# Split products for heads 4 to 11, SP's loads in program order, weights requested six chunks ahead, two weight splits per slot

## Chip, core and metric

The kernel runs on one core of a Trainium2 chip. The metric is the device time of one execution in microseconds (us). TensorE is called PE here, its weight loads PEld, VectorE DVE, ScalarE ACT, GpSimd POOL and SyncE SP.

## What is computed

Windowed attention with global tokens, followed by a two-layer MLP, all in float32. Eight batches, eight heads of 64; 512 local and 32 global tokens. A local token sees the local tokens within 32 places and all global ones; a global token sees everything.

```python
s_g = scale * q_g @ k_all^T;  out_g = softmax(s_g) @ v_all        # k_all, v_all: global and local
s_l = concat(scale * q_l @ k_g^T, where(|i - j| <= 32, scale * q_l @ k_l^T, -1e9))
out_l = softmax(s_l) @ concat(v_g, v_l)
x = concat(out_g, out_l)                  # 8 * 544 tokens, 512 wide
h = maximum(x @ w_in, 0)                  # w_in 512 x 2048
out = (h * h) @ w_out                     # w_out 2048 x 512
```

## The kernel before

**Slots.** The attention is cut into 128 "heads": one head of one batch over one half (256) of its local queries. The loop over t (line 587) handles one head per slot: scores, softmax, transposes of the probabilities, the product with V, and the copy into x. Sixteen heads (two halves of eight) belong to one batch. The MLP follows LAG = 9 slots behind: slot t does step m = t - 9, an eighth of DFF (256 columns) for a block of 256 tokens: gemm1 into h, relu and square, gemm2 into o. Block 0's GEMM reads xg, block 1's x_h and x_l, and so on. In this order block 0 is the group of the first eight heads of batch 0; its eight steps stand in slots 9 to 16. A step of block 0 needs heads 0 to 7 in xg and four chunks of weights.

**Plain and split products.** A float32 product is either plain (operands in float32) or split: an operand is written as hi (rounded to float32r) plus lo (the rest), and the products hi*hi, lo*hi, hi*lo are summed. Heads 0 to 15 (`NPLAIN = 16`, `plain(t)`) and block 0's GEMMs are plain in before, everything later is split. For a split head, `split_head` makes hi with a cast on ACT and the rest with subtractions on DVE. In the buffers of the scores the 64 channels of Q and K stand twice, one copy in each half of the 128 partitions; a plain product therefore gives twice the score and is scaled by 0.0625 instead of 0.125, and a split one keeps hi in the lower and lo in the upper copy of K.

**Global queries.** Every four heads `g_load` loads global queries (qr) and spreads them into a tile of zeros: on POOL into qz for plain heads, with a cast on ACT and a subtraction on DVE into qgz for split ones. `g_scores` multiplies it with K into gs, `g_evac` copies gs into sg. Softmax, transposes and product of the global rows follow as jobs in later slots.

**Weights.** w_in and w_out come as 32 chunks wr of 512 KB in which each float32 number is stored in the two halves of an int64. A chunk is put together by an absolute-value pass on ACT (`w_abs`, ACTIVATE wf<-wr) and two bit passes on DVE (`w_bits`, TENSOR_SCALAR and SCALAR_TENSOR_TENSOR wf); each letter b in `PLAN` is one of a chunk's two bit passes. It is then split into whi and wlo (tile ws, one cast on ACT and one subtraction on DVE) for the blocks after the first: each letter s is one. `PLAN[t]` has four places in slot t. `w_start` asks for chunks up to `LOOK` ahead of the one that is being put together. Weights and plain heads share one pool of 32 buffers of 4 KB per partition.

**Sizes of loads.** A head (raw) is 432 KB, of head 0 first 304 and then 128; half of the masks (con) is 224 KB, the identity 64, the global queries qr 64, a chunk 512.

**What sets the order.** `InOrder` wraps an engine's calls and asks the scheduler to keep them in program order where its flag is on. PE, DVE and ACT get that flag from slot 17 (`FREE`). Before that, and for SP throughout in before, the scheduler chooses an order by its own estimate of times when the kernel is built. On the chip each engine then runs its instructions in the order that was chosen, and waits at an instruction whose operands aren't there.

Of the kernel before, what the change touches and what calls it, by code (L numbers as in the profile page):

```python
# [16 lines left out]
P = 128  # L17
# [10 lines left out]
NPLAIN = 16  # L28

PLAN = [",,,b", "b,,,b", "b,,,b", "b,,b,", "b,,b,", "b,,b,", "b,,b,", "b,b,,b", "b,b,,b", "bb,bb,bb,bb", "bb,bb,bb,bb", "bbs,bb,bbs,bbs", "bbs,bbs,bbs,bbs", "bbs,bbs,bbs,bbs", "bbs,bbs,bs,s", "ss,s,s,s", "ss,s,s,s", "s,,s,", "s,,s,", "s,,s,", "s,,s,", "s,,s,", "s,,s,"]  # L30
FREE = (17, 17, 17)
LOOK = 2
# [26 lines left out]
def attention_moe(  # L59
# [10 lines left out]
    pe, ve, ac = InOrder(tc, nc.tensor), InOrder(tc, nc.vector), InOrder(tc, nc.scalar)  # L70
    PSUM = bass.MemoryType.PSUM
# [12 lines left out]

    w_bufs = {"free": WCH}
# [4 lines left out]
    def load_head(t):  # L90
        if plain(t):
            w_take(1)
            raw = wp.tile([P, 1024], F32, tag="w", name=f"raw{t}")[:, :PK]
        else:
            raw = p2.tile([P, PK], F32, tag="raw", name=f"raw{t}")
        if t == 0:
            nc.sync.dma_start(raw[:, : QC + KC], pk[t, :, : QC + KC])
        else:
            nc.sync.dma_start(raw, pk[t])
        heads[t] = dict(raw=raw)  # L100
# [162 lines left out]
    def g_load(t):  # L263

        b, grp = t // 16, (t // 4) % 2

        def cols(z, j):
            return bass.AP(z.tensor, z.offset + 64 * j, [list(z.ap[0]), [256, 2], [160, 2], [1, 32]])

        src = qg[b, grp].rearrange("p (a b) n -> p a b n", a=2)  # L270
        if plain(t):
            qz = p1.tile([P, 512], F32, tag=("ph", "gvl", "gvh", "ph")[t // 4], name=f"qz{t}")
            nc.gpsimd.memset(qz, 0.0)
            qr = p1.tile([P, 2, 2, 32], F32, tag="qr", name=f"qr{t}")
            (nc.sync if t else nc.scalar).dma_start(qr, src)
            nc.gpsimd.tensor_copy(cols(qz, 0), qr)
        else:
            qz = qgz
            qr = p1.tile([P, 2, 2, 32], F32, tag="qr", name=f"qr{t}")
            nc.sync.dma_start(qr, src)  # L280
            ac.copy(cols(qgz, 0), qr)
            ve.tensor_sub(cols(qgz, 1), qr, f(cols(qgz, 0)))
        state["qz"] = qz

    def g_scores(t):
# [4 lines left out]
        kk = hd["raw" if plain(t) else "hi"]  # L290
# [8 lines left out]
    def g_evac(t):  # L299
        grp, pair = (t // 4) % 2, (t % 4) // 2  # L300
        gs = state["gs"]
        early = plain(t)
# [7 lines left out]
    def g_load_v(t, pair):  # L310
        gv = p1.tile([P, 640], F32, tag="gv", name=f"gv{t}_{pair}").rearrange("p (c n) -> p c n", c=5)
        src = vg[t // 16, 2 * ((t // 4) % 2) + pair]
        nc.sync.dma_start(gv, src.rearrange("(c p) n -> p c n", p=P))
        state["gv"] = gv
# [11 lines left out]
    def g_soft(t):  # L326
# [174 lines left out]
    def evac(blk, tiles=(0, 1)):  # L501
        for i in tiles:
# [76 lines left out]
    for t in range(4, 8):  # L579
# [3 lines left out]
        if t == 6:  # L583
            nc.sync.dma_start(con[:, half:], consts[:, half:])
    scores(0)
    jobs = {}
    for t in range(NSTEP + LAG + 1):
# [40 lines left out]
        if early and t + 1 < NPLAIN:  # L628
            scores(t + 1)
# [11 lines left out]
        if t + 1 < NT:  # L641
# [126 lines left out]
```

## Time and profile before

| | before |
|---|---|
| median of 3 runs (us) | 1073.42 (1073.36 to 1074.84) |
| the profiled execution (us) | 1073.67 |
| its span, first to last instruction (us) | 1071.9 |
| PE, PEld busy (us) | 1055.3, 939.3 |
| DVE, ACT busy (us) | 856.9, 752.2 |
| granted PE clock | 1.0 throughout |

Busy times are sums over instructions of one engine. A matmul's end is modelled in them, and PE works on several at once, so a busy PE may still have room: what PE really takes for a piece is the distance to the next start, as the chain of waits gives it. In a timeline row stand the start, the length, the engine, the line, the operation with its output and inputs, and how many instructions were merged; a plain float32 matmul is two rows. Line 52 is the wrapper of `InOrder`, so operations are told apart by their tiles: s and gs scores, pt transposes, xa and gxo attention products, h and o the two GEMMs.

### The profile page before, as it was taken

Reading aid. Unit: us, or ns where it says so; the run is one execution under the profiler, and the core shown is the slowest. Engines: PE = TensorE matmul, PEld = TensorE weight load, DVE = VectorE, ACT = ScalarE, POOL = GpSimd, SP = SyncE. Lnnn points to the kernel's source line nnn. Section 1 sums busy time; section 2 is a strip of 40 time slices with the busy share of each in tenths; the row PEclk is TensorE's granted clock in tenths of the full one; section 3 lists DMA queues with packets and bytes.
Section 4 is the critical chain, followed back from the end, with each engine's and each line's share of the span. In section 5 each row is a group of like instructions: output and inputs, shape, how many; then the busy total and the mean of one; then the engine's idle time right before and its main releaser. Section 6 shows DMA issues by size and latency. Waiting matters only on the chain.

```text
span 1071.9 us, 21142 instructions
## 1 busy us (share of the span) xinstructions
PE 1055.3 (98%) x7568; PEld 939.3 (88%) x7568; DVE 856.9 (80%) x2687; ACT 752.2 (70%) x1901; POOL 3.9 (0%) x14
## 2 busy tenths in 40 slices
PE   7999999999999999999999999999999999999998
PEld 5676789998999899999998989998999999999896
DVE  4689889888888888888888889888888888884321
ACT  5789776778767776777777776777777787774322
POOL 1000000000000000000000000000000000000000
PEclk9999999999999999999999999999999999999999
DMA  9662222232322222223222222222322322201000
GB/s 372 265 256 92 83 82 82 75 91 76 93 70 82 85 82 66 89 66 102 75 90 65 84 84 82 76 79 83 94 74 69 87 93 65 88 29 34 13 20 20
DMA packets 54312, 96.78 MB, mean 90 GB/s; under 512 B 4288, under 2 KB 29376, under 8 KB 54208
## 3 DMA queue, kind: packets, MB, share of 16 engines
q1 hardware_dynamic: 53632, 94.95, 27.1%
q8 instruction: 60, 0.98, 0.4%
q10 hardware_dynamic: 576, 0.49, 0.2%
q14 instruction: 44, 0.36, 0.1%
HBM read 86.51 MB, written 8.91 MB: 89 GB/s over the span
## 4 chain that ended last, share of the span: by engine, by line
PE 88%; ACT 5%; DVE 3%; DMA 3%; issue 1%; SPq 0%
PE o L52 34%; PE h L52 33%; PE xa L52 7%; PE s L52 5%; PE pt L52 5%; PE gxo L52 2%; PE gs L52 2%; DMA wr<-in_w_dram 1%; DVE prob L52 1%; ACT r L52 1%; ACT ph L52 1%; DMA raw<-in_pk_dram 1%; ACT prob L52 1%; PE gt L52 1%; ACT hi L52 1%
## 5 line engine op out<-in xcount | busy, mean ns | idle before, releaser
L52 PE MATMUL h<-x_h,ws 128*128 128x256 f32 x2048 | 388.8, 283 | 0.0
L52 PEld LDWEIGHTS h<-x_h,ws 128*128 128x128 f32 x2048 | 327.0, 191 | 0.5
L52 PE MATMUL o<-ws,gh 128*128 128x512 f32 x1024 | 321.3, 395 | 0.0
L52 PE MATMUL h<-x_l,ws 128*128 128x256 f32 x1024 | 289.1, 282 | 0.1
L52 PEld LDWEIGHTS o<-ws,gh 128*128 128x128 f32 x1024 | 185.5, 188 | 34.6
L52 PE MATMUL o<-ws,gl 128*128 128x512 f32 x512 | 202.6, 396 | 0.0
L52 PEld LDWEIGHTS h<-x_l,ws 128*128 128x128 f32 x1024 | 195.8, 191 | 0.9 <-DVE x_l L52 0.4
L52 ACT CAST ph<-pt 128x256 fp32r<-128x256 f32 x448 | 141.1, 341 | 68.1 <-PE pt L52 61.2
L52 ACT ACTIVATE prob<-prob,st 128x224 f32<-128x224 f32 x270 | 127.7, 476 | 62.1 <-DVE st L52 60.1
L52 ACT ACTIVATE r<-h 128x512 f32<-128x512 f32 x136 | 81.4, 599 | 112.4 <-PE h L52 112.3
L52 PEld LDWEIGHTS o<-ws,gl 128*128 128x128 f32 x512 | 96.2, 188 | 22.7
L52 DVE CUSTOM_DVE_ANT_0 prob<-s,con 128x224 f32<-128x224 f32 x256 | 89.8, 386 | 25.6 <-PE s L52 19.5
L52 DVE TENSOR_TENSOR gl<-r,gh 128x512 fp32r<-128x512 f32 x128 | 87.9, 686 | 22.3 <-ACT gh L52 20.5
L52 ACT CAST hi<-raw 128x864 fp32r<-128x864 f32 x112 | 102.5, 915 | 1.3
L52 DVE TENSOR_TENSOR r<-h,r 128x512 f32<-128x512 f32 x82 | 56.7, 692 | 52.3 <-ACT r L52 51.0
L52 PE MATMUL xa<-ph,hi 128*64 128x128 f32 x448 | 87.3, 238 | 1.6 <-DVE ph L52 1.2
L52 DVE TENSOR_TENSOR hi<-raw,hi 64x352 fp32r<-64x352 f32 x224 | 82.5, 368 | 6.5
L52 ACT CAST gh<-r 128x512 fp32r<-128x512 f32 x128 | 79.1, 618 | 8.9 <-DVE r L52 8.6
L52 DVE TENSOR_TENSOR ph<-pt,ph 64x128 fp32r<-64x128 f32 x224 | 79.6, 356 | 7.0
L52 DVE TENSOR_TENSOR lo<-raw,hi 128x448 fp32r<-128x448 f32 x112 | 69.7, 622 | 15.2 <-ACT hi L52 12.5
L52 PE MATMUL pt<-con,prob 128*128 128x128 f32 (+1 forms) x512 | 77.9, 274 | 0.1
L52 DVE TENSOR_SCALAR prob<-prob,st 128x224 f32<-128x224 f32 x242 | 70.5, 334 | 4.2
(80 smaller groups left out, 1570.4 us busy)
## 6 DMA issues: line engine op xcount, KB each, us to landing
raw<-in_pk_dram SPq DMA_DIRECT2D x127, 432.0 KB, 3.3
wr<-in_w_dram SPq DMA_DIRECT2D x32, 512.0 KB, 7.4
gv<-in_vg_dram SPq DMA_DIRECT2D x32, 320.0 KB, 3.2
out_dram<-ot SPq DMA_DIRECT2D x32, 256.0 KB, 2.2
qr<-in_qg_dram SPq DMA_DIRECT2D x31, 64.0 KB, 2.7
out_dram<-ot SPq DMA_DIRECT2D x8, 64.0 KB, 1.7
raw<-in_pk_dram SPq DMA_DIRECT2D x1, 304.0 KB, 4.1
con<-in_consts_dram ACTq DMA_DIRECT2D x1, 224.0 KB, 3.9
```

The lines of the kernel that those rows point to most:

```text
L52: r = method(*args, **kwargs)
```

## The change

Heads 4 to 11 (`SCORES`) make their scores and group scores from split operands; their values and the product with V stay plain (`whole(t)` is plain without these heads). Their `split_head` works on 608 columns instead of 864 and is called one slot ahead of the head, right before the scores. Their group queries are qgz on ACT and DVE instead of qz on POOL, and `g_evac` adds two halves on DVE for them; for whole heads it multiplies by 0.5, so that all rows of sg have the same scale. SP's calls go through `InOrder` with its flag always on. `LOOK` is 6 instead of 2. `PLAN` gives two letters s per slot in slots 11 to 14, where 3, 4, 4 and 4 stood, and goes on with two per slot through slot 23 instead of 22.

```diff
+SCORES = range(4, 12)
-PLAN = [..., "bbs,bb,bbs,bbs", "bbs,bbs,bbs,bbs", "bbs,bbs,bbs,bbs", "bbs,bbs,bs,s", "ss,s,s,s", "ss,s,s,s", "s,,s,", ...]
+PLAN = [..., "bbs,bb,bbs,bb", "bbs,bb,bbs,bb", "bbs,bb,bbs,bb", "bbs,bb,b,s", "ss,s,s,s", "ss,s,s,s", "s,,s,", ...]
-LOOK = 2
+LOOK = 6
...
+    sp = InOrder(tc, nc.sync)
...
+    def whole(t):
+        return plain(t) and t not in SCORES
...
-            nc.sync.dma_start(raw, pk[t])
+            sp.dma_start(raw, pk[t])
...
-        if plain(t):
+        if whole(t):
             return
         hi = p2.tile([P, PK], F32R, tag="hi", name=f"hi{t}")
         lo = p2.tile([P, QC + 192], F32R, tag="lo", name=f"lo{t}")
-        ac.copy(hi, raw)
-        ve.tensor_sub(lo, raw[:, KC : KC + QC + 192], f(hi[:, KC : KC + QC + 192]))
+        e = KC + QC if plain(t) else PK
+        n = min(e - KC, QC + 192)
+        ac.copy(hi[:, :e], raw[:, :e])
+        ve.tensor_sub(lo[:, :n], raw[:, KC : KC + n], f(hi[:, KC : KC + n]))
         ve.tensor_sub(hi[64:, :KC], raw[64:, :KC], f(hi[64:, :KC]))
-        ve.tensor_sub(hi[32:64, PK - 64 :], raw[32:64, PK - 64 :], f(hi[32:64, PK - 64 :]))
+        if not plain(t):
+            ve.tensor_sub(hi[32:64, PK - 64 :], raw[32:64, PK - 64 :], f(hi[32:64, PK - 64 :]))
...
-            if plain(t):
+            if whole(t):
                 pe.matmul(s[:, u, :], hd["raw"][:, qs], hd["raw"][:, ks], start=True, stop=True)
...
-        return 0.0625 if plain(t) else 0.125
+        return 0.0625 if whole(t) else 0.125
...
-        if plain(t):
+        if whole(t):
             qz = p1.tile([P, 512], F32, tag=("ph", "gvl", "gvh", "ph")[t // 4], name=f"qz{t}")
...
-        kk = hd["raw" if plain(t) else "hi"]
+        kk = hd["raw" if whole(t) else "hi"]
...
-            ac.copy(dst, gs[:64, cols] if early else gs[64:, cols])
+            if early:
+                ac.activation(out=dst, in_=gs[:64, cols], func=AF.Copy, scale=0.5)
+            else:
+                ac.copy(dst, gs[64:, cols])
...
         if early and t + 1 < NPLAIN:
+            split_head(t + 1)
             scores(t + 1)
...
-        if t + 1 < NT:
+        if NPLAIN <= t + 1 < NT:
             split_head(t + 1)
```

What the scheduler makes of it stands in the built programs. In their rows the number right behind a tile's name is the head, the chunk or, for gs, the first head of a pair; the number behind the underscore only tells buffers apart.

SP's loads behind head 3, before:

```order
L99 DMA raw4_104<-in_pk_dram 128x864
L404 DMA wr0_106<-in_w_dram 128x1024
L404 DMA wr1_108<-in_w_dram 128x1024
L584 DMA con_78<-in_consts_dram 128x448
L99 DMA raw5_112<-in_pk_dram 128x864
L99 DMA raw6_114<-in_pk_dram 128x864
L99 DMA raw7_117<-in_pk_dram 128x864
L99 DMA raw8_122<-in_pk_dram 128x864
```

and now:

```order
L53 DMA raw4_104<-in_pk_dram 128x864
L53 DMA wr0_106<-in_w_dram 128x1024
L53 DMA wr1_108<-in_w_dram 128x1024
L53 DMA wr2_110<-in_w_dram 128x1024
L53 DMA wr3_112<-in_w_dram 128x1024
L53 DMA wr4_114<-in_w_dram 128x1024
L53 DMA wr5_116<-in_w_dram 128x1024
L53 DMA raw5_120<-in_pk_dram 128x864
L53 DMA raw6_122<-in_pk_dram 128x864
L53 DMA con_78<-in_consts_dram 128x448
L53 DMA raw7_125<-in_pk_dram 128x864
L53 DMA raw8_130<-in_pk_dram 128x864
```

Four more chunks stand ahead of heads 5 to 8, and con behind head 6.

PE behind the transposes of head 3 (pt<-prob1), before:

```order
L52 MATMUL s6_302<-raw6_114 128x224 x2
L52 MATMUL s7_337<-raw7_117 128x224
L52 MATMUL xa3_266<-pts3_251,raw3_86 64x256
L52 MATMUL xa3_266<-pts3_251,raw3_86 64x128 x2
L52 MATMUL pt_95<-con_78,prob0_93 128x128 x2
L52 MATMUL pt_95<-con_78,prob0_93 96x128 x2
L52 MATMUL s7_337<-raw7_117 128x224
L52 MATMUL h0_425<-xg_90,wf0_110 128x256
```

and now, from the attention product of head 5 on:

```order
L53 MATMUL xa5_362<-pts5_347,raw5_120 64x256
L53 MATMUL xa5_362<-pts5_347,raw5_120 64x128 x2
L53 MATMUL gs4_278<-hi4_238,qgz_92 128x288
L53 MATMUL gs4_278<-hi5_284,qgz_92 128x288
L53 MATMUL s6_328<-hi6_323 128x224
L53 MATMUL s6_328<-hi6_323,lo6_324 128x224
L53 MATMUL s6_328<-hi6_323 128x224
L53 MATMUL s6_328<-hi6_323,lo6_324 128x224
L53 MATMUL gs6_360<-hi6_323,qgz_92 128x288
L53 MATMUL s7_371<-hi7_366 128x224
```

The scores of heads 6 and 7, ahead of the attention product of head 3 before, stand behind that of head 5 now, and behind the group scores of heads 4 and 5, which read qgz.

DVE behind the probabilities of head 5 (TENSOR_SCALAR prob1), before:

```order
L52 TENSOR_SCALAR prob1_94<-prob1_94,st5_287 128x224 x2
L52 ISA prob0_93,st6_320<-s6_302,con_78 128x224
L52 ISA st6_320 128x1
L52 ISA prob0_93,st6_320<-s6_302,con_78 128x224
L52 ISA st6_320 128x1
L52 TENSOR_SCALAR st6_320<-st6_320 128x2
```

and now:

```order
L53 TENSOR_SCALAR prob1_94<-prob1_94,st5_308 128x224 x2
L53 TENSOR_SCALAR wf2_198<-wf2_198 128x512
L53 SCALAR_TENSOR_TENSOR wf2_198<-wr2_110,wf2_198 128x512
L53 TENSOR_SCALAR wf2_198<-wf2_198 128x512
L53 SCALAR_TENSOR_TENSOR wf2_198<-wr3_112,wf2_198 128x512
L53 TENSOR_SCALAR wf4_276<-wf4_276 128x512
L53 TENSOR_TENSOR qgz_92<-qr4_254,qgz_92 128x2x2x32
L53 SCALAR_TENSOR_TENSOR wf4_276<-wr4_114,wf4_276 128x512
L53 TENSOR_SCALAR wf4_276<-wf4_276 128x512
L53 SCALAR_TENSOR_TENSOR wf4_276<-wr5_116,wf4_276 128x512
L53 TENSOR_TENSOR lo6_324<-raw6_122,hi6_323 128x256
L53 TENSOR_TENSOR hi6_323<-raw6_122,hi6_323 64x352
```

The bits of chunks 2 to 5, qgz and the split of head 6 now stand between head 5's probabilities and the scan (ISA) of head 6's scores.

More of the change, by code (lines that the diff above doesn't have):

```diff
@@ L28 @@
 NPLAIN = 16
-PLAN = [",,,b", "b,,,b", "b,,,b", "b,,b,", "b,,b,", "b,,b,", "b,,b,", "b,b,,b", "b,b,,b", "bb,bb,bb,bb", "bb,bb,bb,bb", "bbs,bb,bbs,bbs", "bbs,bbs,bbs,bbs", "bbs,bbs,bbs,bbs", "bbs,bbs,bs,s", "ss,s,s,s", "ss,s,s,s", "s,,s,", "s,,s,", "s,,s,", "s,,s,", "s,,s,", "s,,s,"]
+SCORES = range(4, 12)
+PLAN = [",,,b", "b,,,b", "b,,,b", "b,,b,", "b,,b,", "b,,b,", "b,,b,", "b,b,,b", "b,b,,b", "bb,bb,bb,bb", "bb,bb,bb,bb", "bbs,bb,bbs,bb", "bbs,bb,bbs,bb", "bbs,bb,bbs,bb", "bbs,bb,b,s", "ss,s,s,s", "ss,s,s,s", "s,,s,", "s,,s,", "s,,s,", "s,,s,", "s,,s,", "s,,s,", "s,,s,"]
 FREE = (17, 17, 17)
-LOOK = 2
+LOOK = 6
 SQ = (2, 3, 4, 5, 14, 15)
@@ L96, in load_head @@
         if t == 0:
-            nc.sync.dma_start(raw[:, : QC + KC], pk[t, :, : QC + KC])
+            sp.dma_start(raw[:, : QC + KC], pk[t, :, : QC + KC])
         else:
-            nc.sync.dma_start(raw, pk[t])
+            sp.dma_start(raw, pk[t])
         heads[t] = dict(raw=raw)
@@ L274, in g_load @@
             qr = p1.tile([P, 2, 2, 32], F32, tag="qr", name=f"qr{t}")
-            (nc.sync if t else nc.scalar).dma_start(qr, src)
+            (sp if t else nc.scalar).dma_start(qr, src)
             nc.gpsimd.tensor_copy(cols(qz, 0), qr)
@@ L279, in g_load @@
             qr = p1.tile([P, 2, 2, 32], F32, tag="qr", name=f"qr{t}")
-            nc.sync.dma_start(qr, src)
+            sp.dma_start(qr, src)
             ac.copy(cols(qgz, 0), qr)
@@ L301, in g_evac @@
         gs = state["gs"]
-        early = plain(t)
+        early = whole(t)
         parts = ((0, 0, 288),) if (t // 8) % 2 == 0 else ((288, 0, 160), (448, 192, 96))
@@ L312, in g_load_v @@
         src = vg[t // 16, 2 * ((t // 4) % 2) + pair]
-        nc.sync.dma_start(gv, src.rearrange("(c p) n -> p c n", p=P))
+        sp.dma_start(gv, src.rearrange("(c p) n -> p c n", p=P))
         state["gv"] = gv
@@ L329, in g_soft @@
         ve.tensor_reduce(out=st[:, 0:1], in_=s[:, :544], op=ALU.max, axis=AX.X)
-        ve.tensor_scalar(out=st[:, 1:2], in0=st[:, 0:1], scalar1=-scale(t), scalar2=None, op0=ALU.mult)
+        ve.tensor_scalar(out=st[:, 1:2], in0=st[:, 0:1], scalar1=-0.125, scalar2=None, op0=ALU.mult)
         state["gst", t] = st
@@ L334, in g_exp @@
         s, st = sg[:, (t // 4) % 2, :544], state["gst", t]
-        ac.activation(out=s, in_=s, func=AF.Exp, scale=scale(t), bias=st[:, 1:2], accum_out=st[:, 2:3])
+        ac.activation(out=s, in_=s, func=AF.Exp, scale=0.125, bias=st[:, 1:2], accum_out=st[:, 2:3])
     def g_norm(t):
@@ L403, in w_load @@
         r = wp.tile([P, 1024], F32, tag="w", name=f"wr{i}")
-        nc.sync.dma_start(r.bitcast(I32), w[i].bitcast(I32))
+        sp.dma_start(r.bitcast(I32), w[i].bitcast(I32))
         wraw[i] = r.rearrange("p (n w) -> p n w", w=2)
@@ L508, in evac @@
                 r0 = b * 544 + 32 + hf * 256 + i * P
-                nc.sync.dma_start(out[r0 : r0 + P, :], ot)
+                sp.dma_start(out[r0 : r0 + P, :], ot)
             else:
@@ L512, in evac @@
                     r0 = (4 * i + bb) * 544
-                    nc.sync.dma_start(out[r0 : r0 + 32, :], ot[32 * bb : 32 * bb + 32, :])
+                    sp.dma_start(out[r0 : r0 + 32, :], ot[32 * bb : 32 * bb + 32, :])
     w_next = {"load": 0, "bits": 0, "split": 0}
@@ L583, in attention_moe @@
         if t == 6:
-            nc.sync.dma_start(con[:, half:], consts[:, half:])
+            sp.dma_start(con[:, half:], consts[:, half:])
     scores(0)
```

## The prediction

> **What bounds the kernel now.** I read the page's engine shares first, then the busy time in stretches of the start, then PE's waits there, then the chain of work in one slot.
>
> ```profile
> span 1071.9 us, 21142 instructions
> core 0: us, PE busy (x) PEld busy (x) DVE busy (x) ACT busy (x) POOL busy (x), PEclk, DMA share, GB/s
> 20.00:30.00 10.00, 9.65 (x56) 7.18 (x56) 6.65 (x35) 7.39 (x23) 0.29 (x1) 1.00 1.03 411
> 30.00:40.00 10.00, 9.60 (x50) 6.74 (x49) 7.74 (x34) 8.54 (x25) 0.59 (x2) 1.00 1.04 406
> ...
> PE s L52 <- DMA raw<-in_pk_dram: 4.9, 1, 4.9
> ...
> PE xa L52 <- DVE ph L52: 1.1, 7, 0.2
> PE s L52 <- ACT sg L52: 0.9, 6, 0.2
> ...
> 59.99 3.43 PE o L52 x8
> 63.42 0.44 PE pt L52 x4
> 63.86 1.73 PE h L52 x8
> 65.58 0.49 PE gs L52 x2
> 66.07 1.73 PE h L52 x8
> 67.80 1.01 PE xa L52 x6
> 68.81 0.95 PE s L52 x4
> ```
>
> The first row of waits is PE's only one for a load in the first 50 us, at the very start; the next two are all its waits behind 190 us, 2.0 us together. The last seven rows are the chain through slot 11. They add up to 9.78 us with no gap: from the first GEMM slots onwards PE sets the pace, and whatever lets the first GEMM begin later moves all that follows by as much. Before that, heads 0 to 7 must go through softmax into xg. In that stretch no engine is full (DVE 6.65 and 7.74 of 10, ACT 7.39 and 8.54) while the DMA engines are (share 1.03, 411 GB/s). So the start is made of waits in a chain, not of work on PE, and the order of the built program decides it.
>
> **Products of heads 4 to 11.** A plain score pair or group score costs what the slot above shows (s 0.95, gs 0.49 us); a split one costs what later slots show:
>
> ```profile
> 103.66 0.44 PE s L52 x4
> 125.41 0.13 PE gs L52
> ```
>
> That saves about 0.5 + 0.36 us of PE a head. Only what stands behind the first output product (o) counts in full, since PE is the bound from there. That is the group score of head 11, 0.36 us. (The group scores of whole heads leave ACT with a factor now instead of none, which is the same pass: nothing, or the width of a reading either way.) The rest lies in the stretch that the next part walks through. Where PE is the bound from about 31 us, as in the second rival, the three scores and eight group scores behind that point give 3 x 0.5 + 8 x 0.36 = 4.4 us.
>
> **The order in the start: the term that decides.** The rows that price the steps are the groups of the first 190 us, with their mean ns behind the comma:
>
> ```profile
> L52 DVE SCALAR_TENSOR_TENSOR wf<-wr,wf 128x512 int32<-128x512 int32 x32 | 22.0, 688 | 0.5
> L52 DVE TENSOR_SCALAR wf<-wf 128x512 int32<-128x512 int32 x32 | 13.8, 431 | 9.5 <-ACT wf L52 9.2
> L52 DVE TENSOR_TENSOR hi<-raw,hi 64x352 fp32r<-64x352 f32 x11 | 5.7, 522 | 0.3
> L52 DVE TENSOR_TENSOR pl<-pt,ph 128x256 fp32r<-128x256 f32 x10 | 4.2, 421 | 0.1
> L52 DVE CUSTOM_DVE_ANT_0 prob<-s,con 128x224 f32<-128x224 f32 x54 | 19.4, 386 | 15.8 <-PE s L52 10.3 <-PE pt L52 5.3
> L52 DVE TENSOR_SCALAR prob<-prob,st 128x224 f32<-128x224 f32 x40 | 11.6, 334 | 0.6
> ...
> L52 ACT ACTIVATE prob<-prob,st 128x224 f32<-128x224 f32 x68 | 31.8, 477 | 19.1 <-DVE st L52 18.8
> L52 ACT ACTIVATE wf<-wr 128x512 f32<-128x512 f32 x32 | 21.4, 669 | 1.2 <-DMA wr<-in_w_dram 1.2
> L52 ACT CAST ws<-wf 128x512 fp32r<-128x512 f32 x32 | 18.6, 615 | 0.0
> L52 ACT COPY pts<-pt 128x512 f32<-128x512 f32 x16 | 9.3, 580 | 2.9 <-PE pt L52 2.8
> L52 ACT CAST gvh<-gv 128x640 fp32r<-128x640 f32 x4 | 2.9, 723 | 0.0
> ```
>
> Neighbours on DVE and ACT overlap by some 0.08 us (below, 0.42 us from 31.73 and the next from 32.07), so I count a chunk's bits on DVE as 1.05, its absolute value on ACT as 0.6, and the split of a head as 0.65 on ACT (608 columns, between the ws and gvh rows) and 0.9 on DVE (the 128x256 and 64x352 rows). A step to another engine counts 0.1.
>
> ```profile
> 31.73 0.42 DVE L52 TENSOR_SCALAR wf<-wf 128x512 int32<-128x512 int32 x1
> 32.07 0.38 DVE L52 CUSTOM_DVE_ANT_0 prob<-s,con 128x224 f32<-128x224 f32 x1
> ...
> 23.09 1.30 PE L52 MATMUL s<-raw 128*128 128x224 f32 x6
> ...
> 25.34 0.66 PE L52 MATMUL pt<-con,prob 128*128 128x128 f32 x4
> ...
> 30.69 0.79 PE L52 MATMUL pt<-con,prob 128*128 128x128 f32 x4
> ...
> 37.78 0.43 PE L52 MATMUL xa<-pts,raw 128*64 128x128 f32 x2
> ...
> 50.05 3.60 PE L52 MATMUL o<-wf,r 128*128 128x512 f32 x8
> ```
>
> These are the marks of before: scores of head 6 from 23.09 (a product in plain float32 is two rows), transposes of head 4 at 25.34, of head 6 at 30.69, the last attention product of head 7 ending at 38.2, the first output product at 50.05. Now the same marks in the changed order:
>
> - Up to head 4's transposes the rows are nearly the same, and its split fits into gaps of ACT and DVE: 25.1.
> - Head 5's scores now stand behind head 4's attention product. Copy of the transposes, cast, two subtractions: 28.0. Softmax, with 2 x 0.386 on DVE, 2 exponentials on ACT, 2 x 0.334 on DVE and the small steps between, takes 3.7: transposes at 31.7.
> - Head 6's scores stand on PE behind the group scores of heads 4 and 5, which now wait for DVE's half of qgz. On DVE both qgz and head 6's split stand behind the bits of chunks 2 to 5. ACT delivers the first of these at 33.55 (pts and two absolute values); DVE then needs 4 x 1.05 + 0.25 for qgz + 0.9 for head 6: 38.95, and the scores run at 39.05. Before, they ran at 23.09, ahead of all this. (qgz is 128 columns, so under the 0.33 us that 224 columns take in the prob row.)
> - Until head 6's probabilities are ready DVE runs through a group sum 0.4 (288 columns, near the 0.42 of the 256 above), head 7's split 0.9, head 6's scan 0.75 and its factor 0.15, head 8's split 0.9, half of chunk 6's bits 0.43, head 7's scan 0.75, three small steps 0.3, the other half 0.6, the product 0.58: 5.76 us, so 44.7. Before: 30.69 for the transposes.
> - Another 3.3 us of DVE of the same kinds to head 7's probabilities, 48.05; ACT has chunks 8 and 9, half of head 8's exponentials, xg and the second qgz ahead of the copy; head 7's attention product ends at 51.1, against 38.2.
> - Until the first o PE has 8.6 us of work (4.3 of h0 and h1 and the rest in scores, transposes and products of heads 8 to 11), with ACT's order (three absolute values, a cast, pts, exponentials, r and its square, x_h, the multiplication on ACT) holding it up in two places by some 3.2 us: 62.85, against 50.05.
>
> The term is **+12.8 us**. Bounds: with another 8% of overlap on the 26 us that DVE and ACT carry in it, and no time for steps between engines, 9; with 0.2 instead of 0.1 for each of about 20 steps, 15. Behind PE's waiting group score stand all scores from head 6 on; DVE's scans wait for those, and h0 for head 7.
>
> **Loads.** SP issues six chunks before heads 5 to 8, instead of two.
>
> Four chunks of 512 KB at 411 GB/s are 5.1 us. From the first landing at 4.9 us, the 5,500 KB up to and with head 5 are here by 18.6, and heads 6 to 9, with half of con and 1,950 KB in all, by 23.5. The walk needs head 5 at 26 and the others later, so this costs nothing in it; it would cost up to 5.1 if that slack were gone. The Trainium skill's page "Perfetto Trace Analysis", section Roofline, says that a lone core is bounded by its 16 DMA engines at about 435 GB/s; the trace's 411 and 406 GB/s at a share of 1.03 and 1.04 agree with the ceiling. By that rule alone the start would be loading-bound and would pay the 5.1 us; the first rival below takes this up.
>
> **Splits later.** Slots 11 to 14 lose seven splits. They are bound by PE (9.78 above), so nothing is won. Slots 21 to 23 get two each that were done by slot 20 before; one more in slot 17 finds room.
>
> ```profile
> 136.79:146.57 9.78, 1.38 (x2) 1.00 0.33 100
> ...
> 128.17:136.79 8.62, 7.96 (x59) 7.14 (x58) 8.12 (x26) 7.81 (x20) 0.00 (x0) 1.00 0.18 53
> 136.79:146.57 9.78, 9.08 (x70) 7.66 (x69) 8.73 (x26) 7.72 (x19) 0.00 (x0) 1.00 0.33 100
> 146.57:154.10 7.53, 7.53 (x59) 6.87 (x58) 6.22 (x22) 5.88 (x15) 0.00 (x0) 1.00 0.31 102
> 154.10:161.46 7.36, 7.36 (x57) 6.73 (x56) 6.62 (x22) 5.34 (x13) 0.00 (x0) 1.00 0.18 61
> 161.46:169.50 8.04, 8.04 (x69) 7.45 (x68) 7.64 (x23) 5.24 (x14) 0.00 (x0) 1.00 0.33 98
> ```
>
> The first row is DVE's part of ws alone in slot 20: two splits are 1.38 us. The others are slots 19 to 23. Added to DVE's 6.22, 6.62 and 7.64 they make 7.60, 8.00 and 9.02 in slots of 7.53, 7.36 and 8.04: over by 0.07, 0.64 and 0.98, together 1.7. With 1.2 for a pair that overlaps its neighbours it is 1.3; with the half microsecond that DVE idles in slot 19 beside 8.12 of work, in each, 3.2. I take **+2.0**, near the first.
>
> **The sum.** 12.8 - 0.4 + 2.0 = 14.4. The profiled execution took 1073.67 us (span 1071.9 and 1.8 around it), 0.25 above the median shown. So 1073.67 + 14.4 = **1088**.
>
> **Rivals.**
> 1. *Only the loads count.* Heads 5 to 8 come 5.1 us later and everything else flows at its old pace: 1073.7 + 5.1 - 0.4 + 2.0 = 1080.4. For it: DMA share 1.03. Against it: in before PE waits for a head's load only at 4.9 us, and the heads had landed long before their scores. Chance 0.10.
> 2. *Faster.* The engines' queues hold nothing up: bits and splits are done early enough that PE is full from about 31 us as now, and the cheaper products come through: 1073.7 - 4.4 + 1.3 = 1070.6. It decides where head 6's scores run: by about 26 us it wins, from 30 us on the start is later than now. For it: DVE and ACT are idle a quarter of the time there. Against it: that idle time is waiting, and each engine in the trace runs its instructions as they stand in the program. The Trainium skill says this outright in "PSUM — Partial Sum Buffer", section Engine vs sequencer instructions: the queues of ScalarE and VectorE are strict FIFO and matmuls start in program order; by that rule the forecast holds, without it this rival would. Chance 0.10.
> 3. *Nothing to see*: a loss of about 4 us in the start given back by the products: 1074. Chance 0.03.
>
> **Chances and range.** The forecast has 0.77. Its bounds are 1073.7 + 9 - 0.4 + 1.3 = 1083.6 and 1073.7 + 15 - 0.4 + 3.2 = 1091.5. I take the range down to the first rival, 1079, and a little up, to 1093. Slower by over 0.2% (about what a measurement of this kernel can tell from no change) 0.87, within it 0.03, faster 0.10.
>
> **What would show it.** Right: transposes of head 6 past 42 us, an idle PE between 28 and 48 us waiting for DVE (qgz, hi), the first o past 59 us, slots 10 to 16 unchanged at 9.8 us, slots 21 to 23 longer by 0.3 to 1 us each with DVE near full. Wrong: scores of head 6 waiting for raw (first rival), or the first o at or before 50 us (second). Wrong too if slots behind 24, which I leave as they are, change: SP's program order puts qr and gv elsewhere among the head loads there, and I count that as nothing because PE waits only 2.0 us in all behind 190 us now.

## The result and the profile after

| | before | after |
|---|---|---|
| median of 4 runs each, side by side (us) | 1073.41 (1073.36 to 1074.84) | 1100.28 (1100.01 to 1101.0) |
| ratio, 95% interval | | 1.0248 (1.023 to 1.0266) |
| span of the profiled execution (us) | 1071.9 | 1098.2 |
| its granted clock | 1.0 | 0.989 |

The change costs 26.9 us. The forecast was slower by 14.4, with a range up to 1093: the sign was right and the size too small. To see where the time came from, I take the start of each slot, that is of its first transposes (pt) on PE, in both traces, and look where the distance between the two grows:

| place | distance grows by (us) | forecast (us) |
|---|---|---|
| start, up to slot 12 (63.26 before, 74.39 after) | 11.1 | 12.8 - 0.4 |
| slot 14 | 1.6 | 0 |
| slot 20 | 5.4 | 0 |
| slots 21 to 23 (all of it in 23) | 1.8 | 2.0 |
| slot 24 | 5.4 | 0 |
| slots 25 to 137, about 0.01 each | 1.0 | 0 |
| sum, the difference of the spans | 26.3 | 14.4 |

First the start. The busy time in the two stretches that the prediction showed of before, then PE's waits before 80 us (in all, times, longest), then rows of PE's timeline (in brackets the idle time ahead of a row and what ended it); all of the changed kernel:

```profile
20.00:30.00 10.00, 5.30 (x30) 3.41 (x30) 5.60 (x21) 6.00 (x17) 0.00 (x0) 0.99 1.03 411
30.00:40.00 10.00, 5.02 (x17) 3.41 (x17) 7.20 (x18) 5.18 (x10) 0.00 (x0) 0.50 1.03 401
```

```profile
PE s L53 <- DMA raw<-in_pk_dram: 4.9, 1, 4.9
PE xa L53 <- ACT pts L53: 3.6, 5, 0.8
PE pt L53 <- DVE prob L53: 3.5, 4, 2.9
PE s L53 <- DVE hi L53: 2.4, 2, 1.8
PE gs L53 <- DVE qgz L53: 1.8, 1, 1.8
```

```profile
23.91 0.79 PE L53 MATMUL pt<-con,prob 128*128 128x128 f32 x4 [0.17 <-DVE prob L53]
27.12 0.34 PE L53 MATMUL s<-hi 128*128 128x224 f32 x1 [0.60 <-DVE hi L53]
30.65 1.15 PE L53 MATMUL pt<-con,prob 128*128 128x128 f32 x4 [2.85 <-DVE prob L53]
36.30 0.85 PE L53 MATMUL gs<-hi,qgz 128*128 128x288 f32 x2 [1.80 <-DVE qgz L53]
38.94 0.52 PE L53 MATMUL s<-hi 128*128 128x224 f32 x1 [1.80 <-DVE hi L53]
44.24 0.79 PE L53 MATMUL pt<-con,prob 128*128 128x128 f32 x4 [0.27 <-DVE prob L53]
61.52 3.60 PE L53 MATMUL o<-wf,r 128*128 128x512 f32 x8
```

PE's busy time in 20 to 30 us falls from 9.65 to 5.30 and in 30 to 40 from 9.60 to 5.02, while the DMA share stays within 0.01. The timeline follows the walk of the prediction: head 4's transposes at 23.9 (forecast 25.1), head 5's scores at 27.1 (28.0), its transposes at 30.65 (31.7), head 6's scores behind the group scores of head 4 at 38.9 (39.05), its transposes at 44.2 (44.7), the first output product at 61.5 (62.85). One thing in the first fence I had not thought of: PE's clock is 0.50 in the second stretch.

Now the slots that the prediction left out. Busy time by slot, 20 to 25, of the changed kernel; then the row of SP that asked for the query rows of slot 20 in before, SP's rows in the changed kernel (SPq is SP's DMA queue), what SP waited for from 147 to 151 us, the rows of ACT, DVE and PE behind them, and from the chain of waits the twelve output products of slot 20 and, as a measure, of a later slot:

```profile
149.55:164.77 15.22, 11.11 (x70) 9.42 (x69) 9.90 (x28) 8.95 (x21) 0.00 (x0) 0.78 0.12 33
164.77:172.09 7.32, 7.32 (x58) 6.72 (x56) 6.37 (x22) 6.39 (x17) 0.00 (x0) 1.00 0.36 110
172.09:179.44 7.35, 7.35 (x56) 6.71 (x55) 6.54 (x20) 6.00 (x15) 0.00 (x0) 1.00 0.20 60
179.44:189.25 9.81, 8.84 (x69) 7.61 (x67) 8.91 (x25) 5.64 (x15) 0.00 (x0) 1.00 0.14 47
189.25:201.96 12.71, 9.52 (x57) 8.09 (x56) 8.55 (x27) 6.38 (x16) 0.00 (x0) 0.87 0.26 75
201.96:209.24 7.28, 7.28 (x55) 6.69 (x54) 6.07 (x19) 4.96 (x14) 0.00 (x0) 1.00 0.20 63
```

```profile
67.47 0.33 SPq L280 DMA_DIRECT2D qr<-in_qg_dram  x1
...
149.87 0.34 SPq L53 DMA_DIRECT2D raw<-in_pk_dram  x1
150.26 0.43 SPq L53 DMA_DIRECT2D qr<-in_qg_dram  x1
...
SPq L53 <- DVE hi L53: 6.2, 1, 6.2
...
153.30 0.30 ACT L53 CAST qgz<-qr 128x128 fp32r<-128x128 f32 x1 [4.50 <-DMA qr<-in_qg_dram]
153.64 0.29 DVE L53 TENSOR_TENSOR qgz<-qr,qgz 128x128 fp32r<-128x128 f32 x1 [3.35 <-ACT qgz L53]
156.20 0.34 PE L53 MATMUL xa<-ph,hi 128*64 128x128 f32 x1 [2.21 <-DVE ptl L53]
158.36 0.37 PE L53 MATMUL xa<-pl,hi 128*64 128x128 f32 x1 [1.71 <-DVE pl L53]
...
159.91 4.24 PE o L53 x12
...
221.19 2.80 PE o L53 x12
```

Slot 20 takes 15.22 us where it took 9.78, slot 24 12.71 where it took 7.30. The query rows qr of the group that begins with head 20 are asked for at 150.26 us, inside the slot that needs them; before, that load went out at 67.47, almost 70 us ahead of its cast on ACT (136.07). SP stood at the load of a head (raw) for 6.2 us until DVE had finished with a buffer (hi), and only then came to qr, which needs 3 us to land. ACT's cast of qr waits 4.5 us for it, DVE's half of qgz 3.35 behind the cast, and everything queued behind these two on ACT and DVE, the split probabilities of the previous head among them, reaches PE late: 2.21 and 1.71 us of idle PE. Then the output products take 4.24 us instead of 2.80, since the clock is halved. 2.21 + 1.71 + 1.44 = 5.4, as much as slot 20 lost (smaller shifts beside these cancel). Slot 24 repeats this with a qr issued at 190.19. From slot 28 on the query rows are in time again, though SP's order is the same: those of group 28 go out at 217.16 us, 6.7 ahead of their slot.

Slot 14, too, was forecast unchanged. PE waits there once, for the part pth of the global rows' probabilities:

```profile
98.28 0.75 PE L53 MATMUL gs<-raw,qz 128*128 128x288 f32 x2 [1.46 <-DVE pth L53]
```

### The profile page after: what moved, and what is told of

Same layout as the page of the kernel before. It is cut to its first block, busy times and chain, and to the rows that moved or that the text cites. A ratio compares the mean times of both kernels' runs of the same rounds, so it can differ in the third digit from the quotient of the medians.

```text
span 1098.2 us, 21141 instructions
## 1 busy us (share of the span) xinstructions
PE 1061.7 (97%) x7560; PEld 941.9 (86%) x7560; DVE 866.5 (79%) x2711; ACT 757.1 (69%) x1911; POOL 2.4 (0%) x10
## 4 chain that ended last, share of the span: by engine, by line
PE 80%; ACT 9%; DVE 6%; DMA 2%; issue 1%; SPq 0%; ACTq 0%; POOL 0%; DVEq 0%; POOLq 0%
PE o L53 31%; PE h L53 29%; PE xa L53 6%; PE s L53 5%; PE pt L53 4%; PE gxo L53 2%; ACT prob L53 2%; PE gs L53 2%; DVE prob L53 2%; ACT r L53 1%; DMA qr<-in_qg_dram 1%; ACT hi L53 1%; ACT ph L53 1%; DVE ws L53 1%; ACT ws L53 1%
## 5 line engine op out<-in xcount | busy, mean ns | idle before, releaser
L53 ACT ACTIVATE prob<-prob,st 128x224 f32<-128x224 f32 x270 | 127.5, 476 | 61.7 <-DVE st L53 59.6
L53 DVE CUSTOM_DVE_ANT_0 prob<-s,con 128x224 f32<-128x224 f32 x256 | 89.6, 386 | 29.2 <-PE s L53 27.1
L53 ACT CAST hi<-raw 128x864 fp32r<-128x864 f32 (+1 forms) x120 | 107.9, 900 | 3.8 <-PE gs L53 2.4
L53 DVE TENSOR_TENSOR hi<-raw,hi 64x352 fp32r<-64x352 f32 x232 | 86.8, 374 | 6.6
L53 DVE TENSOR_TENSOR lo<-raw,hi 128x448 fp32r<-128x448 f32 (+1 forms) x120 | 73.3, 611 | 16.9 <-ACT hi L53 14.0
L53 PEld LDWEIGHTS pt<-con,prob 128*128 128x128 f32 (+1 forms) x512 | 58.9, 134 | 19.4 <-DVE prob L53 4.7
```

The lines of the kernel that those rows point to most:

```text
L53: r = method(*args, **kwargs)
```

## Experiments

All runs are compared with a run of the kernel before beside them. "Start" is how much later slot 12 begins than in the profiled execution of before (63.26 us), and a slot's number is how much longer it is. The expectations call the first output product (o) the first down projection, gemm1 (h) the gate projections and a transposed tile turned; they write TensorE and VectorE for PE and DVE.

| run | time - before (us) | first o at | start | slot 14 | slot 20 | slot 23 | slot 24 |
|---|---|---|---|---|---|---|---|
| the change | 26.9 | 61.5 | 11.1 | 1.6 | 5.4 | 1.8 | 5.4 |
| e1_whole | 16.6 | 52.3 | 3.7 | 0 | 5.7 | 1.8 | 5.5 |
| e2_scores_alone | 13.8 | 62.3 | 11.9 | 2.0 | 0 | 0 | 0 |
| e3_sp_free | 16.0 | 61.7 | 11.3 | 1.5 | 0 | 1.8 | 0.3 |
| e4_plan_of_before | 19.9 | 62.4 | 12.0 | 1.4 | 5.8 | 0 | 0 |
| f1_qr_ahead | 17.3 | 61.5 | 11.1 | 1.8 | 0 | 1.8 | 0.3 |
| f2_more_hi | 27.2 | 63.2 | 12.8 | 2.2 | 4.9 | 1.8 | 4.9 |
| f3_qr4_early | 23.8 | 59.9 | 9.5 | 0.8 | 5.1 | 1.8 | 5.2 |
| f4_scores_8_11 | 2.2 | 48.1 | 1.4 | 0.5 | 0 | 0 | 0 |
| g1_filled_waits | 27.4 | 62.2 | 11.8 | 1.6 | 5.6 | 1.8 | 5.2 |
| g2_six_ahead_alone | 3.3 | 52.8 | 4.2 | -0.1 | 0 | 0 | 0 |
| g3_sp_order_alone | 6.1 | 49.9 | 0.3 | -0.1 | 5.6 | 0 | 0 |
| g4_scores_12_15 | 2.9 | 49.6 | -0.8 | 1.8 | 0 | 0 | 0 |
| h1_group_whole | 5.4 | 54.7 | 4.6 | 1.9 | 0 | 0 | 0 |
| h2_no_low_part | 7.8 | 56.3 | 6.3 | 0.6 | 0 | 0 | 0 |

Where o's first eight products are split by other work, the column gives the first of them; the start by slot 12 is then the safer mark. Not in the table: 0.85 us in slot 25 of e3 and f1, and 1.8 in slot 13 of g4.

### Which part of the change does what

```diff
# e1_whole: from the changed kernel
-SCORES = range(4, 12)
+SCORES = range(0)
# e2_scores_alone: from the changed kernel, the other three parts undone
-LOOK = 6
+LOOK = 2
-    sp = InOrder(tc, nc.sync)
+    sp = nc.sync
# (and PLAN of before)
# e3_sp_free: from the changed kernel
-    sp = InOrder(tc, nc.sync)
+    sp = nc.sync
# e4_plan_of_before: from the changed kernel, PLAN of before
```

> The changed kernel, but heads 4 to 11 keep whole products (SP's program order, the weights asked for six chunks ahead and the new plan stay). Theory: the start of the changed kernel is late because the scores of heads 6 and 7 stand behind the group scores of head 4 on the TensorE (two buffers for a head's split halves), and the waits of slots 20 and 24 are SP's program order, which this kernel keeps. Then the first down projection starts within 1.5 us of 50.05 us (61.52 in the changed kernel), slots 20 and 24 stay 5 us longer than before, slot 23 1.8 us, and the time is 1085 to 1089 us. Rival: the start is late because six chunks of weights are asked for ahead of heads 5 to 9; then the first down projection stays past 56 us and the time is 1094 to 1101 us.

Measured 1090.94 us, ratio 1.0157 (1.0128 to 1.0187), 1.9 us above the theory's range and 3.1 below the rival's. The marks decide: the first output product starts at 52.25 us, 2.2 later than before and 9.3 earlier than in the changed kernel, so most of the loss of the start goes with the split products; slots 20, 23 and 24 keep their losses. The 3.7 us that the start still loses were on neither list.

> The kernel before with the split products of heads 4 to 11 alone (SP unordered, two chunks ahead, the plan of before). Theory: the whole loss of the start is here, 10 to 12 us, with the first down projection at 60 to 62 us, and slots 20 and 24 are as before: 1083 to 1087 us. Rival (the loads make the start late): first down projection within 3 us of 50.05 and 1073 to 1077 us.

Measured 1088.12 us, 1.0131 (1.0102 to 1.0161). The theory holds in its marks (the first output product at 62.28, 0.3 past its range; slots 20 and 24 as before). Slot 14's wait is here too, 2.0 us, and the time is 1.1 us more than expected. So the start and slot 14 belong to the split products.

> The changed kernel with SP's loads left to the scheduler again. Theory: the query rows of groups 20 and 24 are asked for late only because SP issues them behind the load of a head that waits for its buffer; without the order they are issued more than 10 us before their use, slots 20 and 24 lose their 5.4 us each, the first down projection stays at 61.5 us: 1088 to 1091 us. Rival (the late query rows come of their own buffer, or of VectorE's late splits): 1098 to 1101 us with the waits for qr in slots 20 and 24 still there.

Measured 1090.29 us, 1.0151 (1.0122 to 1.0181), inside the theory's range. Slot 20 is back at its old length and slot 24 within 0.3 us of it; the query rows of groups 20 and 24 go out at 95.2 and 150.7 us.

> The changed kernel with the plan of before (three splits in the slots of bits, the last split in slot 22 and not 23). Theory: one of the two buffers of head loads is held by the last weight chunk until its split; with that split one slot sooner the load ahead of the query rows of group 24 finds a buffer in time, so slot 24 loses its 5.4 us and slot 23 its 1.8 us, while slot 20's 5.4 us stay: 1091 to 1095 us. Rival (the order on SP alone delays both, whatever the buffer): slot 24 keeps 5 us, 1097 to 1100 us.

Measured 1094.19 us, 1.0188 (1.0158 to 1.0217). Slots 23 and 24 lose nothing, slot 20 keeps 5.8: the theory, but for the slot that it names. The last chunk wf31 lives in one of the two buffers of head loads until its split. Under the plan of before this split runs in slot 20, not 22 (the letters that stand in slots 21 and 22 find nothing left to split; the same holds for g3 below). Under the new plan it stands in slot 23 and runs when PE is already in slot 24. Each time SP's next load of a head follows at once; first e4, then the changed kernel:

```profile
161.33 0.69 DVE L53 TENSOR_TENSOR ws<-wf,ws 128x512 fp32r<-128x512 f32 x1
162.10 0.33 SPq L53 DMA_DIRECT2D raw<-in_pk_dram  x1
...
194.74 0.69 DVE L53 TENSOR_TENSOR ws<-wf,ws 128x512 fp32r<-128x512 f32 x1
195.50 0.33 SPq L53 DMA_DIRECT2D raw<-in_pk_dram  x1
```

Until then SP's load of a head in front of the query rows has one buffer to take turns in. In e4 there are two again in time for group 24: that load goes out earlier, and the query rows follow at 181.13 us, 7.5 ahead of the slot. Slot 20 lies in the time with one buffer under either plan. That its loss, too, needs the occupied buffer fits slot 28, where the same order costs nothing, but no run tests it. Where SP is unordered (e3), the new plan leaves 1.8 us in slot 23, 0.3 in slot 24 and 0.85 in slot 25; the 5.4 of slot 24 need SP's order too.

### SP's order by itself

```diff
# f1_qr_ahead: from the changed kernel; g_ask is the load of qr from g_load
+        if t % 4 == 3 and NPLAIN <= t + 1 < NT:
+            state["qr", t + 1] = g_ask(t + 1)
         if NPLAIN <= t + 2 < NT:
             load_head(t + 2)
# g3_sp_order_alone: from the kernel before
+    sp = InOrder(tc, nc.sync)   # and all nc.sync below it
# g2_six_ahead_alone: from the kernel before
-LOOK = 2
+LOOK = 6
```

> The changed kernel, SP still in program order, but from slot 15 on the query rows of the next group are written ahead of the load of head t+2 in the last slot of a group, instead of behind it. Theory: only the place behind the head's load made them late, so slots 20 and 24 lose their 5.4 us each, while the start stays (first down projection at 61.5 us) and slot 23 keeps its 1.8 us: 1088 to 1091 us. Rival (any order on SP makes some load late here, the head's load then takes the place of the query rows): 1095 us or more, with a wait for a head's hi or raw in slots 21 and 25.

Measured 1091.14 us, 1.0162 (1.0133 to 1.0192), 0.1 above the theory's range. SP stays in program order, and 64 KB are asked for one place earlier. SP's row in slot 19, and slot 20 from its start in stretches of 3.4 us:

```profile
145.88 0.43 SPq L53 DMA_DIRECT2D qr<-in_qg_dram  x1
...
149.69:153.10 3.41, 3.23 (x28) 2.97 (x27) 3.29 (x9) 2.61 (x8) 0.00 (x0) 1.00 0.48 130
153.10:156.50 3.40, 3.25 (x25) 2.76 (x24) 2.66 (x10) 2.66 (x7) 0.00 (x0) 1.00 0.00 0
```

The load leaves 4.4 us earlier than in the changed kernel, PE is busy for 95% of these stretches and keeps its clock. That is the whole of slot 20 and all but 0.3 us of slot 24: not the bytes or the engine, but what stands in front of one small load on a queue that waits in order.

> The kernel before with SP's loads in program order alone (two chunks ahead, plan of before, last split in slot 22). Theory: slot 20 loses 5 to 6 us to its query rows, slot 24 nothing, since the last chunk's buffer is free by then, and the start is within 1 us of before: 1078 to 1081 us. Rival (with two chunks ahead SP reaches the head loads earlier, and the query rows of group 20 are in time): 1073 to 1075 us.

Measured 1080.01 us, 1.0057 (1.0037 to 1.0077): 5.6 us in slot 20, nothing in slot 24, 0.3 in the start, as the theory says, save that the last split runs in slot 20.

> The kernel before with the weights asked for six chunks ahead alone. Theory: the 3.7 us that the start loses with whole products are the loads of heads 5 to 9 standing behind four more chunks; they are all here, nothing else changes: slot 11 begins 3 to 4.5 us later than before and 1076 to 1079 us. Rival (they came of SP's order or the plan): slot 11 within 1 us of before, 1072.5 to 1075 us.

Measured 1077.23 us, 1.0028 (1.0016 to 1.004): 4.2 us in the start and nothing behind it, about what was left over in e1. The time and the place are the theory's; its reason isn't seen in the trace. PE waits for a load of a head only at 4.9 us, as before. Head 5's load goes out at 9.88 us, and no load of a head in the first 40 us takes more than 9.5 us to land, so it is there by 19.4. Its scores run at 26.28 us, because the built order has them behind the transposes of head 4; before, they ran from 19.77. So its transposes wait for their probabilities and start at 30.66 us instead of 27.75. What the chip loses here is a matter of order, then; that the scheduler chose this order because it reckoned with later loads is likely but not shown. Behind split products the same loads add nothing: the start of the change (11.1) is not later than that of e2 (11.9).

### What makes the start late

```diff
# f2_more_hi: from the changed kernel, in split_head, for t < NPLAIN
+        w_take(1)               # w_take(-1) behind the group scores
+        both = wp.tile([P, 1024], F32R, tag="w", name=f"hl{t}")
+        hi, lo = both[:, : QC + KC], both[:, QC + KC : 2 * QC + KC]
# f3_qr4_early: from the changed kernel; g_load uses what is there
+        if t == 1:
+            state["qr", 4] = g_ask(4)
+        if t == 4:
+            state["qr", 8] = g_ask(8)
# g1_filled_waits: from the changed kernel, in transposes(t)
+        for _ in range({5: 16, 6: 12}.get(t, 0)):
+            pe.transpose(pt[:, :P], ident, ident)
```

> The changed kernel with the split halves of heads 4 to 11 in the 32 buffers of the weight chunks instead of two buffers each; loads, SP's order and plan unchanged. Theory A (two buffers hold head 6's halves back until the group scores of head 4 are done): head 6's probabilities are turned by 38 us instead of 44.2, the first down projection starts at 52 to 57 us, slots 20 and 24 keep their 5.4 us each: 1091 to 1096 us. Theory B (the query rows of group 4, landed at 30.5 us, and the bits ahead of them on VectorE decide): the first down projection stays at 60 us or later, 1098 to 1102 us.

Measured 1101.07 us, 1.0255 (1.0225 to 1.0285), first o at 63.16: theory A falls, and time and mark are those of theory B. More buffers alone don't help. With them the scheduler built another order, and the wait moved to head 4, whose split now comes behind the bits of the chunks on ACT and DVE, as the row of its scores shows:

```profile
28.57 1.16 PE L53 MATMUL s<-hl 128*128 128x224 f32 x4 [4.35 <-DVE hl L53]
```

> As the run with the query rows ahead, and those of group 4 are asked for in slot 1 and of group 8 in slot 4, so they land some 10 us earlier; two buffers of split halves as in the changed kernel. Theory A (two buffers decide, and what frees them is the group scores, which wait for these rows): the group scores of head 4 start before 33 us instead of 36.3 and the first down projection 2 to 4 us earlier, 57.5 to 59.5 us; 1085 to 1088 us. Theory B (the rows decide alone): the start falls to within 4 us of before, 1079 to 1082 us. Theory C (neither; the order of VectorE and ScalarE decides): first down projection at 61 us or later, 1089 to 1091 us.

Measured 1097.67 us, 1.0223 (1.0193 to 1.0253). The kernel that ran asked only for the rows of groups 4 and 8 earlier; from group 16 on they stood where the change has them, so slots 20 and 24 kept their 10.3 us and the expected times don't apply. By the marks it is near theory A: head 4's group scores start at 31.67 us instead of 36.30, and the first output product at 59.85, 1.7 earlier. So the query rows are a small part.

> The changed kernel with 28 transposes of the identity added on the TensorE, 16 ahead of the transposes of head 5 and 12 ahead of those of head 6, into columns of the tile pt that the real ones overwrite; they stand in the waits of 2.85 and 1.8 us, and all other instructions keep their order. Theory (the granted clock of 0.5 from 29.84 to 43.49 us comes of the TensorE's idling before it, and the 9 us of matmuls in that stretch at half speed make part of the loss): the clock stays at 1.00 through 45 us, and the first down projection starts 2 to 4.5 us earlier than 61.5. Rival (the low clock costs nothing, since the chain through ScalarE and VectorE sets the end of each head): the clock stays up and the first down projection is within 0.7 us of 61.5, or later by the fillers. In both, slots 20 and 24 keep their 5.4 us: 1095.5 to 1098 by the theory, 1099.5 to 1103 by the rival.

Measured 1101.30 us, 1.0255 (1.0235 to 1.0276). The fillers kept the clock at 1.00 up to 40.9 us; after that it was at 0.50 until 47.7, so the stretch was put off, not removed. Head 6's transposes came at 43.86 us instead of 44.24 in an execution whose head 4 is 0.54 later, so the full clock gained 0.9 us there, and the first output product at 62.16 is no earlier. Time and mark are the rival's. But both expectations took it that the clock would stay up, and 6.8 of the 13.65 us at half clock were still there, only later. So what the clock costs in the start is not settled; up to head 6's transposes it is under 1 us.

Two explanations were left, and the next two runs put them to the test:

```diff
# h1_group_whole: from e2_scores_alone, in g_load, g_scores and g_evac
-        if whole(t):
+        if plain(t):
-        kk = hd["raw" if whole(t) else "hi"]
+        kk = hd["raw" if plain(t) else "hi"]
# h2_no_low_part: from e2_scores_alone, for t < NPLAIN
-        ve.tensor_sub(lo[:, :n], raw[:, KC : KC + n], f(hi[:, KC : KC + n]))
-        ve.tensor_sub(hi[64:, :KC], raw[64:, :KC], f(hi[64:, :KC]))
-                pe.matmul(s[:, u, :], hd["lo"][:, u * P : u * P + P], hd["hi"][:, ks], start=False, stop=True)
```

> As the run with the split products alone (SP unordered, two chunks ahead, plan of before), but the group scores of heads 4 to 11 take the whole rows and whole query rows as before; only the heads' own scores are split. Theory (head 6's halves wait for the buffers that head 4's group scores hold, and these for the split query rows): with nothing but a head's own scores reading its halves, the scores of heads 6 and 7 stand ahead of the group scores again, head 6's transposes begin by 36 us instead of 45.4, the first down projection starts at 51 to 55 us instead of 62.3, and the time is 1075 to 1080 us. Rival (each head's casts and subtractions make the start late): the first down projection stays past 58 us, 1083 us or more.

Measured 1079.59 us, 1.0052 (1.0036 to 1.0069), in the theory's range. Rows of PE: head 6's scores at 26.84 us, ahead of every group score of heads 4 to 7 (first at 35.23), its transposes at 36.32, and the first output product:

```profile
26.84 0.35 PE L53 MATMUL s<-hi 128*128 128x224 f32 x1
...
35.23 1.14 PE L53 MATMUL gs<-raw,qz 128*128 128x288 f32 x4
...
36.32 0.27 PE L53 MATMUL pt<-con,prob 128*128 128x128 f32 x1
...
54.68 3.60 PE L53 MATMUL o<-wf,r 128*128 128x512 f32 x8
```

The start loses 4.6 us instead of 11.9. So 7.3 of the 11.9 hang on the group scores reading the halves and the split query rows. The run takes both away together.

> As the run with the split products alone, but heads 4 to 11 leave out the low halves: one cast, no subtraction, one product instead of two for a head's scores; the group scores read the cast rows and the split query rows as there. The output differs by the left-out products. Theory (the place behind the group scores of head 4 decides): the first down projection stays within 2 us of 62.3, 1085 to 1089 us. Rival (the subtractions on VectorE make the start late): the first down projection is before 56 us and the time below 1082 us.

Measured 1081.95 us, 1.0077 (1.0057 to 1.0097), first o at 56.34: the time is just inside the rival's range, the mark 0.3 us past it. The theory's marks are missed, though its wait is still there. PE still waits for the query rows ahead of head 4's group scores, and head 6's scores still stand behind them:

```profile
34.16 0.53 PE L53 MATMUL gs<-hi,qgz 128*128 128x288 f32 x2 [2.86 <-DVE qgz L53]
35.35 0.77 PE L53 MATMUL s<-hi 128*128 128x224 f32 x2 [0.66 <-ACT hi L53]
```

But without the subtractions the start loses 6.3 us, 5.6 less. The two shares, 7.3 and 5.6, add up to more than 11.9: they overlap, as they would on one chain where taking either away shortens the same waits. Both hold some of the half clock as well: it lasts 17.1 us in the start of e2, 3.4 in h1 and 6.8 in h2.

### Two looks for a gain

```diff
# f4_scores_8_11 and g4_scores_12_15: from e2_scores_alone
-SCORES = range(4, 12)
+SCORES = range(8, 12)     # range(12, 16) in g4
```

> The kernel before with split products in heads 8 to 11 alone (SP unordered, two chunks ahead, plan of before). Theory: the loss lies in slots 4 to 7, where the TensorE waits; heads 8 to 11 are scored when the gate projections already fill its waits, so the first down projection starts within 2 us of 50.05 and the time is 1071 to 1077 us. Rival (each split head costs its extra casts and subtractions wherever it stands, 13.9 us over eight heads): half of it, 1080 to 1083 us.

Measured 1076.07 us, 1.0018 (1.0007 to 1.0029). The loss is not a price per head: four of the eight heads cost 2.2 us. That this is because gemm1 fills PE while they are scored fits, and no run shows it by itself. They don't gain either.

> The kernel before with split products in heads 12 to 15 alone (SP unordered, two chunks ahead, plan of before). Looked at as a way to gain: in slots 11 to 16 the TensorE never waits, so fewer passes for the scores and group scores should shorten them, 0.5 to 1 us a head by the score rows: 1070 to 1072 us. Rival: VectorE, already busy with bits and splits there, gets two more subtractions a head and the TensorE waits for it: 1074 to 1078 us.

Measured 1076.74 us, 1.0027 (1.0016 to 1.0038): the rival. PE comes out up to 1.5 us ahead by slot 13, then loses 1.8 in each of slots 13 and 14. In slot 13 it waits for DVE's x_l, as the rival says. In slot 14 it is busy throughout, but its granted clock is 0.86 on average, and the same sixteen products of gemm1 take 5.30 us where they took 3.62; the last row is that of before:

```profile
83.08 0.66 PE L53 MATMUL gt<-con,sg 128*128 128x128 f32 x4 [2.23 <-DVE x_l L53]
...
83.57:96.12 12.55, 12.55 (x60) 9.07 (x58) 11.80 (x30) 10.83 (x24) 0.00 (x0) 0.86 0.15 47
...
84.12 5.30 PE L53 MATMUL h<-xg,wf 128*128 128x256 f32 x16
...
83.79 3.62 PE L52 MATMUL h<-xg,wf 128*128 128x256 f32 x16
```

So about half of what these two slots lose comes of the clock, which fell behind the wait in slot 13 and which neither expectation names.

No kernel of these runs is faster than the one before.

## Why the prediction was half right

**The start: right, by the steps given.** 11.1 us against 12.4, with each mark of the walk within 1.4 us of the trace; the 0.4 for head 11's group score shows in slot 11, 9.43 us against 9.78. DVE sets the chain as the walk has it: from the first of the four chunks' bits at 33.06 us to the end of head 6's split at 38.79 it pauses only 0.34 us. What I left out is that the halves have two buffers, so head 6's cast waits for head 4's group scores. In the changed kernel that cast ends at 37.64, 0.2 us before DVE comes to it, so it costs nothing here; in e2 DVE waits 0.83 us for it. Taking the group scores off the halves gives back 7.3 us of e2's loss (h1), taking the subtractions off DVE 5.6 (h2), and the two overlap. More buffers alone cure nothing (f2).

**Loads at nothing: right for this kernel.** PE waits for no load of a head behind the first. With whole products six chunks ahead cost 4.2 us (g2), near the 5.1 that I held against the case that the slack is gone, but there too PE waits for no such load: the scheduler's other order makes the start late. The first rival had about this price, by a cause that doesn't show.

**Splits later: right in size.** 1.8 us against 2.0. The working spread it over slots 21 to 23, mostly 23; it is all in slot 23 (9.81 us against 8.05). The chain of waits runs over ACT and DVE from 176 to 190 us, as assumed. Without SP's order 0.3 and 0.85 us more come in slots 24 and 25 (e3).

**SP's order: the step that failed.** The prediction says: "SP's program order puts qr and gv elsewhere among the head loads there, and I count that as nothing because PE waits only 2.0 us in all behind 190 us now." That inference doesn't hold. The waits it goes by begin at 190 us, and the two slots that lost stood at 137 and 169 us in before, where the working looked at DVE only. Nor would a longer stretch have helped: PE's short waits were those of an order in which the scheduler had put qr of group 20 at 67.47 us, almost 70 us ahead of its use. The small waits showed what the old order achieved, and nothing about the new one. What had to be asked is what stands ahead of qr on SP in the new order, and when that can issue. It is a load of a head, and while wf31 holds one of the two buffers, the other comes free only when DVE has split the head before it, at the end of the slot before the one that needs qr. So the term that I put at nothing is 10.9 us in two slots (e3, f1, g3). Slot 24 also needs the later split of wf31 (e4): I priced that split as DVE work and not as a buffer held on from slot 20 into slot 24.

**Slot 14: missed, 1.6 us.** PE waits there 1.46 us for DVE's pth. The wait is in every run with split products in heads 4 to 11 and is absent without (e1, g2, g3); without the subtractions it is 0.6 (h2), with the rows of group 4 earlier 0.8 (f3). That DVE is behind with its work there because of the subtractions fits h2; f3 has them all and still waits less, so they can't be the whole of it. No run was made for it alone, and the cause stays open. The 1.0 us that builds up behind slot 25, some 0.01 us per slot, stays unexplained. It goes with the split halves in their two buffers: the runs that have them show 0.8 to 1.3 us, e1, g2 and g3, without split products, 0.1 to 0.2, and f2, with the halves elsewhere, none.

**The second rival** (PE full from 31 us) is out: PE is busy for half of 20 to 40 us. The third is out with it.

## What to carry to other kernels

When a queue is put into program order, go through it entry by entry and ask of each small load what stands in front of it and which buffer that one waits for; the waits of the old order say nothing about this, because they belong to that order. A buffer that holds something else for a few slots more is a cost of its own, apart from the work that is moved. And where a reader holds the buffers that a chain waits for, taking the reader away helped here (h1), while more buffers did not (f2).

## What the runs showed of the hardware

PE's granted clock fell to one half after short idle times (2.85 us at most in the changed kernel's start), which I had not reckoned with. Stretches of the changed kernel, cut where the clock changes:

```profile
23.02:26.43 3.41, 2.51 (x16) 1.52 (x14) 1.33 (x5) 1.61 (x4) 0.00 (x0) 1.00 1.03 412
26.43:29.84 3.41, 0.77 (x5) 0.52 (x4) 1.41 (x7) 1.40 (x5) 0.00 (x0) 1.00 1.04 408
29.84:33.25 3.41, 1.87 (x6) 1.16 (x7) 1.11 (x5) 1.36 (x3) 0.00 (x0) 0.50 1.03 417
...
40.08:43.49 3.41, 3.41 (x14) 2.85 (x13) 3.23 (x16) 3.06 (x8) 0.00 (x0) 0.50 1.02 410
43.49:46.90 3.41, 3.14 (x16) 2.04 (x16) 3.35 (x14) 3.15 (x9) 0.00 (x0) 1.00 1.02 412
...
152.72:156.13 3.41, 1.27 (x11) 1.06 (x9) 2.19 (x4) 2.77 (x8) 0.00 (x0) 1.00 0.01 3
156.13:159.54 3.41, 1.63 (x10) 1.36 (x11) 2.21 (x9) 2.10 (x7) 0.00 (x0) 0.50 0.00 0
```

The first number behind a stretch's length is PE's busy time, the third from the end the clock. The low clock lasts 13.65 us in the start, 6.83 in slot 20 and 3.41 in slot 24: four, two and one times 3.41. It begins behind a stretch of 3.41 us in which PE was busy for 0.77, 1.27 and 0.73 us, in g1 behind one with 1.66, in g4 behind one with 1.20, and in the changed kernel it ends each time behind one in which PE was busy throughout. What it costs depends on who waits: 1.4 us in slot 20 and 1.7 in slot 14 of g4, where the chain of waits runs over PE, and under 1 us up to head 6's transposes in the start, as far as g1 tells. The Trainium skill's page "TensorE: Matmul & The Clock Gate", section "What's actually happening", tells of a free-running window of 3413 ns whose activity sets the clock to half or full; the lengths here agree. It lets the clock fall after an idle window; here windows in which PE was busy for 21 to 49% were enough.
